# Block-diagonal products of later groups in three one-pass parts, and another way to turn float64 weights into fp32

## The chip, the cores and the metric

The kernel runs on one core of one Trainium2 chip. The metric is the device time of one execution in microseconds (us). The core's engines are PE (matmuls; PEld is its loading of weights), DVE, ACT, POOL (GpSimd) and SP, which here issues the DMAs.

## The reference, cut to what matters

A linear attention block feeds an MLP.

```
kv  = einsum('bhsd,bhse->bhde', k, v)          # (8, 8, 576, 64) inputs
out = einsum('bhsd,bhde->bhse', q, kv)
x   = out / sqrt(mean(out*out, -1) + 1e-6) * g_norm     # -> (4608, 512)
h   = x @ w_in                                  # w_in (512, 2048), float64
g   = h * erf(softplus(h))
y   = g @ w_out                                 # w_out (2048, 512), float64
```

The two weights arrive as float64, two 32-bit words per number. The result is fp32.

## The kernel before, in words

**Groups.** The tokens are handled in nine groups. Groups T = 0 to 7 are the first 512 tokens of each of the eight sequences; the 64 tokens left over from each sequence together make the ninth, T = 8 (`T == B`). The constant FIRST is 2. Heads go in pairs p = 0 to 3: two heads of 64 fill the 128 partitions.

**Attention of one pair** (`attention(T, p)`, L266 and on) is a list of pieces. `products` multiplies k and v into kv_ps (L294), copies the two 64x64 blocks into the block-diagonal matrix bd_kv (L309) and transposes q with PE into qt_ps (L316), which ACT copies to qT in SBUF (L317). `apply` multiplies bd_kv with the tail of q (L321) and with qT (L322, se_ps, an fp32 product), and ACT squares the result (L325). `halve` cuts the square in two fp32r parts (L335, L336). `mean` sums over the heads' rows with PE (L343, L344) and makes the inverse root on ACT by Ln, Exp and Square (L355 to L357); a table load stands ahead of it and one behind it (L103, L106). `norm` makes x with three operations of DVE (L363, L366, L375), the last of which reads se_ps. `split` cuts x into three fp32r forms (L402 on ACT, L405 and L408 on DVE).

**The MLP in three one-pass products.** fp32r products run in one pass. A number is cut into a high and a low part, and a third form holds both with the low part scaled by SHIFT = 4096. `product` (L459) multiplies high by high and low by low into the bank n_ps, and both by both into m_ps; the sum is (SHIFT − 1) n_ps + m_ps, made by one scaled copy from n_ps and one addition of m_ps (L834 on ACT and L442 on DVE for h; L773 or L437 on DVE, and L442, for the result e). `upper`, `lower`, `upper_w` and `lower_w` make these forms; the weights' forms are made once, written to DRAM and read again for each group.

**Stages.** To 29 us: attention of group 0 and the first loads. To about 180 us: group 0's MLP with plain fp32 weights (hidden product L689, result product L517, column n of the 16 hidden columns at a time), while the weights are converted. To about 285 us: group 1, during which the forms of the weights are written out. From there on blocks of 24.9 us: block m = 4T + b takes four hidden columns of group T (the products of `hidden`), then the four result products of the block before it (`result`). The attention of pair b of group T + 1 is threaded in by hand: its pieces are called at the `places` 0 (ahead of the first hidden product), 1 to 4 (behind each of them) and 5 to 8 (behind each result product). Within a block the gates (L873) and the cutting of g (L402, L405, L408 on g_forms) also have fixed places. The program's order is each engine's order: nothing is moved by a scheduler.

**The conversion of the weights** goes in 18 pieces: the first four columns of w_in singly (512 words per partition), the rest of w_in and all of w_out in twos (1024). `load_w` brings a piece to w_raw. `w_split` (L209 to L217) lets ACT scale the upper word, read as fp32, by 2^-112 into w_e (L215), and the lower word by 2^-29 into the integer w_m (L216). `w_join` (L219 to L237) lets DVE shift w_e left by three (L225), put the sign in (L228) and add w_e and w_m as integers (L237); this last is an integer addition that appears in the profile as a custom operation. The pieces of the conversion are called by `weights()` ahead of the column that needs them.

Of the kernel before, what the change touches and what calls it, by code (L numbers as in the profile page):

```python
# [39 lines left out]
FP32 = mybir.dt.float32  # L40
FP32R = mybir.dt.float32r
# [19 lines left out]
def kernel(  # L61
# [110 lines left out]
    for i in range(2):  # L172
        nc.vector.memset(mean_f[i * D : i * D + D, i * D : i * D + D], 1.0 / D)
    nc.vector.tensor_copy(out=mean_w, in_=mean_f)
    eps_col = const.tile([P, 1], FP32, name="eps_col")
    nc.vector.memset(eps_col, EPS)
    bd_kv = const.tile([P, 2, P], FP32, name="bd_kv")
# [19 lines left out]
                in_=moe_w_out.rearrange("(t p) f -> p t f", p=P)[:, f : f + k, :],  # L197
            )

    def words(which, f):  # L200

        raw = w_raw[which, f]
        hi, lo = (
            raw.bitcast(kind).rearrange("p (n two) -> p n two", two=2)[:, :, half]
            for kind, half in ((FP32, 1), (U32, 0))
        )
        return hi, lo, raw.rearrange("p (n two) -> p n two", two=2)[:, :, 1]

    def w_split(which, f, k):  # L209


        hi, lo, _ = words(which, f)
        e = early.tile([P, G * k], I32, name="w_e", tag="w_e", bufs=2)
        m = early.tile([P, G * k], I32, name="w_m", tag="w_m", bufs=2)
        nc.scalar.activation(e.bitcast(FP32), hi, AF.Copy, scale=2.0**-112)  # L215
        nc.scalar.activation(m, lo, AF.Copy, scale=2.0**-29)  # L216
        w_cv[which, f] = e, m  # L217

    def w_join(which, f, k):  # L219


        hi = words(which, f)[2]
        e, m = w_cv.pop((which, f))
        w_raw.pop((which, f))
        nc.vector.tensor_scalar(  # L225
            out=e, in0=e, scalar1=3, scalar2=None, op0=ALU.logical_shift_left
        )
        nc.vector.scalar_tensor_tensor(  # L228
            out=e, in0=hi, scalar=-(1 << 31), in1=e, op0=ALU.bitwise_and, op1=ALU.bitwise_or
        )  # L230
        if which == "in":
            out_ = w_in_sb[:, :, f * P : (f + k) * P]
            e, m = (t.rearrange("p (c f) -> p c f", c=KC) for t in (e, m))
        else:
            out_ = w_out_sb[:, f : f + k, :]
            e, m = (t.rearrange("p (c f) -> p c f", c=k) for t in (e, m))
        nc.vector.tensor_tensor(out=out_.bitcast(I32), in0=e, in1=m, op=ALU.add)  # L237


    w_order = sorted(  # L240
# [25 lines left out]
    def attention(T, p, pools=None):  # L266

        st = {}

        halves = FIRST <= T < B  # L270
        bd = bd_kv[:, (T * NP + p) % 2, :]

        q_tail, o_tail = slice(P, 2 * P), slice(2 * P, 2 * P + R)
# [11 lines left out]
        def products():  # L285

            kv_ps = st["kv"] = bank("kv_ps")
            ks, vs, qs = (x.pop((T, p)) for x in (k_sb, v_sb, q_sb))
            C = chunks(T)
            for c in range(C):  # L290
                rows = slice(0, S // C + (c < S % C))
                for i in range(2):
                    s = slice(i * D, i * D + D)
                    nc.tensor.matmul(  # L294
                        kv_ps[s, s],
                        lhsT=ks[rows, i, c],
                        rhs=vs[rows, i, c],
                        start=(c == 0),
                        stop=(c == C - 1),
                    )  # L300
            if p % 2 == 0:
                nc.tensor.transpose(kv_ps[:, q_tail], q_last[:, p // 2], ident)
            if p == NP - 2:
                for i in range(NP):
                    load_last(T + 1, i)
            st["qT"] = square_tile("qT")
            for i in range(2):
                s = slice(i * D, i * D + D)
                nc.vector.tensor_copy(out=bd[s, s], in_=kv_ps[s, s])  # L309
            if p % 2 == 0:  # L310
                tails[T] = attp.tile([P, P], FP32, name="qT_last", tag="t")
                nc.vector.tensor_copy(out=tails[T], in_=kv_ps[:, q_tail])
            st["tail"] = tails[T][:, p % 2 * R : p % 2 * R + R]
            qt_ps = bank("qt_ps")
            for j in range(J):
                nc.tensor.transpose(qt_ps[:, j * P : j * P + P], qs[:, j], ident)  # L316
            nc.scalar.copy(st["qT"], qt_ps)  # L317

        def apply():
            qT, o_ps, kv_ps = st["qT"], bank("se_ps"), st.pop("kv")  # L320
            nc.tensor.matmul(kv_ps[:, o_tail], lhsT=bd, rhs=st.pop("tail"), start=True, stop=True)  # L321
            nc.tensor.matmul(o_ps, lhsT=bd, rhs=qT, start=True, stop=True)  # L322
            nc.vector.tensor_copy(out=x_last[:, p, T * R : T * R + R], in_=kv_ps[:, o_tail])
            st["o"] = o_ps
            nc.scalar.activation(qT, o_ps, AF.Square)  # L325
# [12 lines left out]
        def mean(table=True):  # L338
            ms = st["ms"] = bank("ms_ps")
            if halves:  # L340


                nc.tensor.matmul(ms, lhsT=mean_w, rhs=st.pop("hi"), start=True, stop=False)  # L343
                nc.tensor.matmul(ms, lhsT=mean_w, rhs=st.pop("lo"), start=False, stop=True)  # L344
                u = square_tile("u")
            else:
                u = st.pop("qT")
                nc.tensor.matmul(ms, lhsT=mean_w.bitcast(FP32), rhs=u, start=True, stop=True)  # L348
            if T > 0:
                r = attp.tile([P, G], FP32, name="rms_r", tag="rms_r")  # L350
                exp_ln_table()
            else:
                r = gate.tile([P, G], FP32, name="rms_r", tag="s")
            st["u"], st["r"] = u, r
            nc.scalar.activation(r, ms, AF.Ln, bias=eps_col)  # L355
            nc.scalar.activation(r, r, AF.Exp, scale=-0.5)
            nc.scalar.activation(u, r, AF.Square)  # L357
            if table and (T > 0 or p == NP - 1):
                softplus_table()

        def norm():
            ms, u, r = (st.pop(name) for name in ("ms", "u", "r"))
            nc.vector.scalar_tensor_tensor(  # L363
                out=u, in0=ms, scalar=EPS, in1=u, op0=ALU.add, op1=ALU.mult
            )
            nc.vector.scalar_tensor_tensor(  # L366
                out=u, in0=u, scalar=3.0, in1=r, op0=ALU.subtract, op1=ALU.mult
            )
            if T < FIRST:
                if T not in xT:  # L370
                    xT[T] = wide.tile([P, KC, G], FP32, name="xT", tag="ab"[T])
                x = xT[T][:, p, :]
            else:
                x = st["x"] = x_new.tile([P, G], FP32, name="x", tag="x")
            nc.vector.scalar_tensor_tensor(  # L375
                out=x,
                in0=st.pop("o"),
                scalar=gm_col,
                in1=u,
                op0=ALU.mult,  # L380
                op1=ALU.mult,
            )
# [9 lines left out]
            return products, apply, halve, mean, norm  # L392
        if T == B:
            return lambda: None, square, lambda: None, mean, norm, split

        pieces = ((products,), (apply,), (halve, loads)) if halves else ((products, loads), (apply,), ())
        return (*(partial(chain, *group) for group in pieces), mean, norm, split)
# [45 lines left out]

    banks = [(ps_h, "h"), (ps_h, "h")] + [(ps_o, f"o{i}") for i in range(4)]

    def product(weights, moving, turns=True):


        n_ps, m_ps = (
            pool.tile([P, G], FP32, name=name, tag=tag)  # L450
            for name, (pool, tag) in zip(("n_ps", "m_ps"), banks[:2])
        )
        if turns:
            banks.extend(banks[:2])
            del banks[:2]
        for ps, forms in ((n_ps, (0, 1)), (m_ps, (2,))):
            for k in range(4):
                for form in forms:
                    nc.tensor.matmul(  # L459
                        ps,  # L460
                        lhsT=weights(form, k),
                        rhs=moving(form, k),
                        start=(form == forms[0] and k == 0),
                        stop=(form == forms[-1] and k == 3),
                    )
        return n_ps, m_ps
# [276 lines left out]

    low_room.close()
    room.close()
    ctx.enter_context(tc.tile_pool(name="shift", bufs=1, side="right")).tile([P, 504], FP32, name="shift")
    late_r = ctx.enter_context(tc.tile_pool(name="late_r", bufs=1, side="right"))
    gate_r = ctx.enter_context(tc.tile_pool(name="gate_r", bufs=1, side="right"))
    w_out_p = ctx.enter_context(tc.tile_pool(name="w_out_p", bufs=7, side="right"))
# [13 lines left out]
    def result(T, b, j, g, w):  # L763
# [5 lines left out]
        if b == 0:  # L769
            if j == 0:  # L770
                all_e = wide.tile([P, J, DM], FP32, name="e", tag="a")
                es.update((i, all_e[:, i]) for i in range(J))
            nc.vector.tensor_scalar(  # L773
                out=es[j], in0=ps[0], scalar1=SHIFT - 1.0, scalar2=None, op0=ALU.mult
            )
        else:
            add_scaled(es[j], ps[0], SHIFT - 1.0)
        add(es[j], ps[1])
# [5 lines left out]
    for m in range(first_batch, batches + 1):  # L784
# [21 lines left out]
                todo[5] = partial(chain, todo[5], softplus_table)  # L806
        elif b == NB - 1:
            places = (0, 2, 3, 5, 6, 7)

        def pieces(place):  # L810
            while todo and places[-len(todo)] <= place:
# [101 lines left out]
```

## Time and profile before

| | |
|---|---|
| median of 16 runs | 981.81 us (980.03 to 984.15) |
| the profiled execution | 981.4 us |
| its span | 979.6 us, 11746 instructions |
| granted PE clock, mean | 0.985 |
| PE busy | 942.1 us, 96% |
| DVE busy | 716.5 us, 73% |
| ACT busy | 617.5 us, 63% |
| DMA | 259.78 MB, mean 265 GB/s |

Times in the profile count from the start of the span. A line of groups names the line of the code, the engine, the operation, output and inputs with partitions by elements; then the number of instructions, their busy time and the mean of one; then the idle time of the engine just before them and what ended it. In a list of windows a stretch is followed by busy time and number of instructions of PE, PEld, DVE, ACT and POOL, and then by the granted PE clock, the DMA engines' share and GB/s. PEclk in the slices is the granted clock in tenths of full speed. A line of waits reads: engine and line, what it waited for, us in total, how often, the longest.

An fp32 128x512 matmul appears as two instructions, and four of them take 3.43 us on the chain; eight one-pass products of fp32r take 1.83 us. Granted clock and PE's waits differ between the early stage and the rest.

### The profile page before, as it was taken

To read this page: it belongs to the slowest core of one execution; us is meant where nothing else is said; L and a number is where in the kernel's file an instruction comes from. 1 tells how busy PE (TensorE), PEld (TensorE's weight loads), DVE (VectorE), ACT (ScalarE), POOL (GpSimd) and SP (SyncE) were. 2 spreads that over 40 slices of the span, in tenths; PEclk is the share of its full clock that TensorE was granted. 3 is DMA by queue.
4 is the path that set the end of the run, shared out by engine and by line. 5 is a ranking of instruction groups with operands and counts; after the bars stand their busy time and mean duration, and the time that the engine had idled before them with its cause. 6 is when DMAs were issued, how large, how long until landed. Compare 5 with 4: busy or idle time off the path is not lost.

```text
span 979.6 us, 11746 instructions
## 1 busy us (share of the span) xinstructions
PE 942.1 (96%) x4272; PEld 687.6 (70%) x4272; DVE 716.5 (73%) x1019; ACT 617.5 (63%) x825; POOL 2.4 (0%) x10
## 2 busy tenths in 40 slices
PE   5578999999999999999999999999999999999997
PEld 4234444566667888887888788777888878888886
DVE  2543654888767888777788787777888877787667
ACT  3665877677666666666666666666666666665551
POOL 0000000000000000000000000000000000000000
PEclk9878999999999999999999999999999999999999
DMA  9754540589979999898988888888888669778871
GB/s 239 238 153 119 169 122 13 208 307 344 327 248 354 311 301 307 282 318 282 300 299 292 292 304 306 290 279 299 288 313 354 257 244 343 266 281 301 335 274 46
DMA packets 111842, 259.78 MB, mean 265 GB/s; under 512 B 43864, under 2 KB 69544, under 8 KB 111784
## 3 DMA queue, kind: packets, MB, share of 16 engines
q1 hardware_dynamic: 110152, 256.73, 76.2%
q10 hardware_dynamic: 1568, 2.29, 0.9%
q8 instruction: 34, 0.56, 0.2%
q14 instruction: 24, 0.20, 0.1%
q0 software_dynamic: 64, 0.00, 0.0%
HBM read 224.40 MB, written 34.60 MB: 264 GB/s over the span
## 4 chain that ended last, share of the span: by engine, by line
PE 86%; DVE 6%; ACT 4%; DMA 2%; issue 1%; SPq 0%; DVEq 0%; ACTq 0%
PE n_ps L459 43%; PE m_ps L459 21%; PE o_ps L517 7%; PE h_ps L689 6%; PE se_ps L322 3%; PE kv_ps L294 2%; PE qt_ps L316 1%; DMA q_last<-in_q_dram 1%; DVE w_e L228 1%; DMA w_in<-w_new 1%; PE ms_ps L348 1%; DMA q_sb<-in_q_dram 1%; DVE w_in_sb L237 1%; ACT w_e L215 1%; DVE h L873 1%
## 5 line engine op out<-in xcount | busy, mean ns | idle before, releaser
L459 PE MATMUL n_ps<-x_forms,w_in_parts 128*128 128x512 f32 x896 | 234.6, 403 | 0.2
L459 PE MATMUL n_ps<-w_out_parts,g_forms 128*128 128x512 f32 x928 | 232.6, 392 | 0.0
L459 PEld LDWEIGHTS n_ps<-w_out_parts,g_forms 128*128 128x128 f32 x928 | 174.2, 188 | 39.7 <-issue 1.7
L459 PEld LDWEIGHTS n_ps<-x_forms,w_in_parts 128*128 128x128 f32 x896 | 166.6, 188 | 45.5 <-issue 10.2
L849 ACT ACTIVATE s<-h 128x512 f32<-128x512 f32 x112 | 71.1, 634 | 177.4 <-DVE h L442 177.4
L459 PE MATMUL m_ps<-w_out_parts,g_forms 128*128 128x512 f32 x464 | 124.4, 390 | 0.0
L442 DVE TENSOR_TENSOR h<-m_ps,h 128x512 f32<-128x512 f32 x116 | 79.7, 687 | 60.7 <-ACT h L834 42.6
L459 PE MATMUL m_ps<-x_forms,w_in_parts 128*128 128x512 f32 x448 | 121.2, 392 | 0.0
L517 PE MATMUL o_ps<-w_out_sb,h_sb 128*128 128x512 f32 x224 | 100.9, 593 | 0.3 <-DVE h_sb L639 0.3
L459 PEld LDWEIGHTS m_ps<-w_out_parts,g_forms 128*128 128x128 f32 x464 | 87.1, 188 | 18.5
L459 PEld LDWEIGHTS m_ps<-x_forms,w_in_parts 128*128 128x128 f32 x448 | 84.1, 188 | 18.9
L689 PE MATMUL h_ps<-xT,w_in_sb 128*128 128x512 f32 x144 | 75.9, 674 | 19.8 <-DVE w_in_sb L237 19.8
L442 DVE TENSOR_TENSOR e<-m_ps,e 128x512 f32<-128x512 f32 x116 | 80.2, 692 | 19.1 <-PE m_ps L459 11.9
L437 DVE SCALAR_TENSOR_TENSOR e<-n_ps,e 128x512 f32<-128x512 f32 x88 | 60.3, 685 | 43.9 <-PE n_ps L459 43.9
L517 PEld LDWEIGHTS o_ps<-w_out_sb,h_sb 128*128 128x128 f32 x224 | 42.5, 191 | 49.4 <-issue 47.0
L408 DVE SCALAR_TENSOR_TENSOR g_forms<-g_forms 128x1024 fp32r<-128x1024 f32 x58 | 71.1, 1225 | 2.0
L689 PEld LDWEIGHTS h_ps<-xT,w_in_sb 128*128 128x128 f32 x144 | 30.1, 215 | 59.7 <-issue 35.3
L405 DVE TENSOR_TENSOR g_forms<-h,g_forms 128x1024 fp32r<-128x1024 f32 x58 | 70.6, 1217 | 1.7 <-ACT g_forms L402 1.4
L834 ACT ACTIVATE h<-n_ps 128x512 f32<-128x512 f32 x112 | 65.5, 585 | 5.3 <-PE n_ps L459 5.3
L873 DVE TENSOR_TENSOR h<-h,s 128x1024 f32<-128x1024 f32 x58 | 68.3, 1218 | 0.6 <-ACT s L853 0.6
L402 ACT ACTIVATE g_forms<-h 128x1024 fp32r<-128x1024 f32 x58 | 58.9, 1060 | 12.7 <-PE m_ps L459 10.0
L106 ACT ACT_TABLE_LOAD x44 | 56.5, 1283 | 0.7
(95 smaller groups left out, 1014.7 us busy)
## 6 DMA issues: line engine op xcount, KB each, us to landing
w_out_parts<-w_out SPq DMA_DIRECT2D x116, 768.0 KB
w_in_parts<-w_in SPq DMA_DIRECT2D x112, 768.0 KB
w_in<-w_new SPq DMA_DIRECT2D x16, 768.0 KB
q_sb<-in_q_dram SPq DMA_DIRECT2D x32, 256.0 KB
w_raw<-in_moe_w_out_dram SPq DMA_DIRECT2D x8, 1024.0 KB
out_dram<-e SPq DMA_DIRECT2D x32, 256.0 KB
k_sb<-in_k_dram SPq DMA_DIRECT2D x28, 287.5 KB
v_sb<-in_v_dram SPq DMA_DIRECT2D x28, 287.5 KB
```

The source lines that it names most:

```text
L106: nc.scalar.preload_act_table_set("softplus")
L402: nc.scalar.activation(high, x, AF.Copy, scale=1.0 + 2.0**-13)
L405: nc.vector.tensor_tensor(out=low, in0=x, in1=high.bitcast(FP32), op=ALU.subtract)
L408: nc.vector.scalar_tensor_tensor(out=both, in0=low.bitcast(FP32), scalar=SHIFT, in1=high.bitcast(FP32), op0=ALU.mult, op1=ALU.add,)
L437: nc.vector.scalar_tensor_tensor(out=out_, in0=ps, scalar=scale, in1=out_, op0=ALU.mult, op1=ALU.add)
L442: nc.vector.tensor_tensor(out=out_, in0=ps, in1=out_, op=ALU.add)
L459: nc.tensor.matmul(ps, lhsT=weights(form, k), rhs=moving(form, k), start=(form == forms[0] and k == 0), stop=(form == forms[-1] and k == 3),)
L517: nc.tensor.matmul(o_ps[j], lhsT=g[:, j * P : j * P + P], rhs=w_out_sb[:, f, :], start=(f == 0), stop=last,)
L689: nc.tensor.matmul(plain[i], lhsT=w_in_sb[:, c, i % FC * P : i % FC * P + P], rhs=xT[T][:, c, :], start=(c == 0), stop=(c == KC - 1),)
L834: nc.scalar.activation(h[:, i], n_ps, AF.Copy, scale=SHIFT - 1.0)
L849: nc.scalar.activation(s[:, i], h[:, i], AF.Softplus)
L873: nc.vector.tensor_tensor(out=part(h, half), in0=part(h, half), in1=part(s, half), op=ALU.mult)
```

## The change

It has four parts. In groups 3 to 7 (the fourth to eighth; `parts`) the product of bd_kv and qT is done like the MLP's, in three one-pass products of cut parts, in two of the banks that the MLP's products turn through. The forms of bd_kv are made by DVE (three operations) in `products`; the copy of qT becomes ACT's `upper`; a new piece `cut` at place 1 lets DVE make the low and the both form; `apply_parts` multiplies, ACT copies (SHIFT − 1) n_ps to a tile o in SBUF, DVE adds m_ps, ACT squares o. `norm` then reads o. In the conversion DVE takes exponent and mantissa out of the upper word, ACT turns them into two floats (Relu with a bias, and Identity), and DVE puts the sign to the exponent's float, adds the lower word scaled by 2^-52 to the mantissa's, and multiplies. In `result` the scaled copy to e in the first block of a group (b == 0) goes from DVE to ACT. The pool `shift` is replaced by the pool of the forms of bd_kv.

```diff
@@ w_split
+        hi = w_raw[which, f].rearrange("p (n two) -> p n two", two=2)[:, :, 1]
-        nc.scalar.activation(e.bitcast(FP32), hi, AF.Copy, scale=2.0**-112)
-        nc.scalar.activation(m, lo, AF.Copy, scale=2.0**-29)
+        nc.vector.tensor_scalar(
+            out=e, in0=hi, scalar1=20, scalar2=0x7FF,
+            op0=ALU.logical_shift_right, op1=ALU.bitwise_and,
+        )
+        nc.scalar.activation(e, e, AF.Relu, scale=float(1 << 23), bias=exp_col)
+        nc.vector.tensor_scalar(
+            out=m, in0=hi, scalar1=0xFFFFF, scalar2=None, op0=ALU.bitwise_and
+        )
+        nc.scalar.activation(m.bitcast(FP32), m, AF.Identity, scale=2.0**-20, bias=1.0)
@@ w_join
-        nc.vector.tensor_scalar(
-            out=e, in0=e, scalar1=3, scalar2=None, op0=ALU.logical_shift_left
-        )
         nc.vector.scalar_tensor_tensor(
             out=e, in0=hi, scalar=-(1 << 31), in1=e, op0=ALU.bitwise_and, op1=ALU.bitwise_or
         )
+        nc.vector.scalar_tensor_tensor(
+            out=m, in0=lo, scalar=2.0**-52, in1=m, op0=ALU.mult, op1=ALU.add
+        )
-        nc.vector.tensor_tensor(out=out_.bitcast(I32), in0=e, in1=m, op=ALU.add)
+        nc.vector.tensor_tensor(out=out_, in0=e, in1=m, op=ALU.mult)
@@ products
+            if parts:
+                kv = st["kv3"] = parts_p.tile([P, 3, P], FP32R, name="kv_forms", tag="kv3")
+                nc.vector.tensor_scalar(
+                    out=kv[:, 0], in0=bd, scalar1=(1.0 + 2.0**-13) / SHIFT, scalar2=None, op0=ALU.mult,
+                )
+                lower_w(bd, *(kv[:, i] for i in range(3)))
...
-            nc.scalar.copy(st["qT"], qt_ps)
+            if parts:
+                x = st["q3"] = [
+                    pool.tile([P, G], FP32R, name=f"q_{name}", tag=tag)
+                    for name, pool, tag in (
+                        ("high", attp, "rms_r"),
+                        ("low", attp, "sq_lo"),
+                        ("both", x_new, "x"),
+                    )
+                ]
+                upper(qt_ps, x[0])
+                st["qt"] = qt_ps
+            else:
+                nc.scalar.copy(st["qT"], qt_ps)
+
+        def cut():
+            lower(st.pop("qt"), *st["q3"])
+
+        def apply_parts():
+            x, w, kv_ps = st.pop("q3"), st.pop("kv3"), st.pop("kv")
+            nc.tensor.matmul(kv_ps[:, o_tail], lhsT=bd, rhs=st.pop("tail"), start=True, stop=True)
+            n_ps, m_ps = two_banks()
+            for i, ps in enumerate((n_ps, n_ps, m_ps)):
+                nc.tensor.matmul(ps, lhsT=w[:, i], rhs=x[i], start=(i != 1), stop=(i != 0))
+            nc.vector.tensor_copy(out=x_last[:, p, T * R : T * R + R], in_=kv_ps[:, o_tail])
+            o = st["o"] = attp.tile([P, G], FP32, name="o", tag="qT")
+            nc.scalar.activation(o, n_ps, AF.Copy, scale=SHIFT - 1.0)
+            add(o, m_ps)
+            st["qT"] = x_new.tile([P, G], FP32, name="sq", tag="x")
+            nc.scalar.activation(st["qT"], o, AF.Square)
@@ attention's list of pieces
+        if parts:
+            return products, cut, apply, partial(chain, halve, loads), mean, norm, split
@@ result
-            nc.vector.tensor_scalar(
-                out=es[j], in0=ps[0], scalar1=SHIFT - 1.0, scalar2=None, op0=ALU.mult
-            )
+            nc.scalar.activation(es[j], ps[0], AF.Copy, scale=SHIFT - 1.0)
@@ the blocks' places
+        if len(todo) > len(places):
+            places = (places[0], 1, *places[1:])
```

The tiles u and x of these groups move to the pool x_new. `two_banks` is the part of `product` that takes two banks, made a function of its own.

More of the change, by code (lines that the diff above doesn't have):

```diff
@@ L174 @@
     nc.vector.tensor_copy(out=mean_w, in_=mean_f)
+    exp_col = const.tile([P, 1], FP32, name="exp_col")
+    nc.vector.memset(exp_col, -896.0 * (1 << 23))
     eps_col = const.tile([P, 1], FP32, name="eps_col")
@@ L198, in load_w @@
             )
[L200 to L205, printed above, removed]
-        )
-        return hi, lo, raw.rearrange("p (n two) -> p n two", two=2)[:, :, 1]
     def w_split(which, f, k):
-        hi, lo, _ = words(which, f)
+        hi = w_raw[which, f].rearrange("p (n two) -> p n two", two=2)[:, :, 1]
         e = early.tile([P, G * k], I32, name="w_e", tag="w_e", bufs=2)
         m = early.tile([P, G * k], I32, name="w_m", tag="w_m", bufs=2)
-        nc.scalar.activation(e.bitcast(FP32), hi, AF.Copy, scale=2.0**-112)
-        nc.scalar.activation(m, lo, AF.Copy, scale=2.0**-29)
+        nc.vector.tensor_scalar(
+            out=e,
+            in0=hi,
+            scalar1=20,
+            scalar2=0x7FF,
+            op0=ALU.logical_shift_right,
+            op1=ALU.bitwise_and,
+        )
[4 more added lines that the diff above has]
+        nc.scalar.activation(m.bitcast(FP32), m, AF.Identity, scale=2.0**-20, bias=1.0)
         w_cv[which, f] = e, m
     def w_join(which, f, k):
[L222 to L225, printed above, removed]
-            out=e, in0=e, scalar1=3, scalar2=None, op0=ALU.logical_shift_left
-        )
+        raw, (e, m) = w_raw.pop((which, f)), w_cv.pop((which, f))
+        hi = raw.rearrange("p (n two) -> p n two", two=2)[:, :, 1]
+        lo = raw.bitcast(U32).rearrange("p (n two) -> p n two", two=2)[:, :, 0]
         nc.vector.scalar_tensor_tensor(
@@ L230, in w_join @@
         )
+        m = m.bitcast(FP32)
+        nc.vector.scalar_tensor_tensor(
+            out=m, in0=lo, scalar=2.0**-52, in1=m, op0=ALU.mult, op1=ALU.add
+        )
+        e = e.bitcast(FP32)
         if which == "in":
@@ L270, in attention @@
         halves = FIRST <= T < B
+        parts = FIRST < T < B
         bd = bd_kv[:, (T * NP + p) % 2, :]
@@ L305, in products @@
                     load_last(T + 1, i)
-            st["qT"] = square_tile("qT")
+            if not parts:
+                st["qT"] = square_tile("qT")
             for i in range(2):
@@ L309, in products @@
                 nc.vector.tensor_copy(out=bd[s, s], in_=kv_ps[s, s])
+            if parts:
+                kv = st["kv3"] = parts_p.tile([P, 3, P], FP32R, name="kv_forms", tag="kv3")
+                nc.vector.tensor_scalar(
+                    out=kv[:, 0],
+                    in0=bd,
+                    scalar1=(1.0 + 2.0**-13) / SHIFT,
+                    scalar2=None,
+                    op0=ALU.mult,
+                )
+                lower_w(bd, *(kv[:, i] for i in range(3)))
             if p % 2 == 0:
@@ L316, in products @@
                 nc.tensor.transpose(qt_ps[:, j * P : j * P + P], qs[:, j], ident)
-            nc.scalar.copy(st["qT"], qt_ps)
+            if parts:
[25 more added lines that the diff above has]
+            nc.scalar.activation(st["qT"], o, AF.Square)
         def apply():
+            if parts:
+                return apply_parts()
             qT, o_ps, kv_ps = st["qT"], bank("se_ps"), st.pop("kv")
@@ L344, in mean @@
                 nc.tensor.matmul(ms, lhsT=mean_w, rhs=st.pop("lo"), start=False, stop=True)
-                u = square_tile("u")
+                u = (
+                    x_new.tile([P, G], FP32, name="u", tag="x")
+                    if parts
+                    else square_tile("u")
+                )
             else:
@@ L372, in norm @@
                 x = xT[T][:, p, :]
+            elif parts:
+                x = st["x"] = u
             else:
@@ L394, in attention @@
             return lambda: None, square, lambda: None, mean, norm, split
+        if parts:
+            return products, cut, apply, partial(chain, halve, loads), mean, norm, split
         pieces = ((products,), (apply,), (halve, loads)) if halves else ((products, loads), (apply,), ())
@@ L444, with two_banks @@
     banks = [(ps_h, "h"), (ps_h, "h")] + [(ps_o, f"o{i}") for i in range(4)]
-    def product(weights, moving, turns=True):
-        n_ps, m_ps = (
+    def two_banks(turns=True):
+        ps = [
             pool.tile([P, G], FP32, name=name, tag=tag)
             for name, (pool, tag) in zip(("n_ps", "m_ps"), banks[:2])
-        )
+        ]
         if turns:
@@ L455, in product @@
             del banks[:2]
+        return ps
+    def product(weights, moving, turns=True):
+        n_ps, m_ps = two_banks(turns)
         for ps, forms in ((n_ps, (0, 1)), (m_ps, (2,))):
@@ L745 @@
     room.close()
-    ctx.enter_context(tc.tile_pool(name="shift", bufs=1, side="right")).tile([P, 504], FP32, name="shift")
+    parts_p = ctx.enter_context(tc.tile_pool(name="parts_p", bufs=1, side="right"))
     late_r = ctx.enter_context(tc.tile_pool(name="late_r", bufs=1, side="right"))
@@ L772, in result @@
                 es.update((i, all_e[:, i]) for i in range(J))
-            nc.vector.tensor_scalar(
-                out=es[j], in0=ps[0], scalar1=SHIFT - 1.0, scalar2=None, op0=ALU.mult
-            )
+            nc.scalar.activation(es[j], ps[0], AF.Copy, scale=SHIFT - 1.0)
         else:
```

## The prediction

> **What bounds the kernel now.** I read the engine shares and the slices first, then the windows by stage, then PE's and DVE's waits, last the order of one block. The page:
>
> ```profile
> PE 942.1 (96%) x4272; PEld 687.6 (70%) x4272; DVE 716.5 (73%) x1019; ACT 617.5 (63%) x825; POOL 2.4 (0%) x10
> ...
> PEclk9878999999999999999999999999999999999999
> ...
> PE 86%; DVE 6%; ACT 4%; DMA 2%; issue 1%; SPq 0%; DVEq 0%; ACTq 0%
> ```
>
> PE is busy 96% of the span and makes 86% of the chain that ends last. That is a mean over two different stages, as the windows show (columns: stretch, then busy time of PE, PEld, DVE, ACT):
>
> ```profile
> 29.00:180.00 151.00, 131.21 (x393) 59.22 (x392) 77.75 (x105) 99.97 (x130) 0.00 (x0) 0.91 0.42 132
> ...
> 300.50:500.00 199.50, 199.50 (x1014) 160.26 (x1013) 159.91 (x228) 126.65 (x168) 0.00 (x0) 1.00 0.90 301
> ```
>
> From 300.5 us on, PE never idles: 8 blocks in 199.5 us, 24.94 us a block, with 20.0 of DVE and 15.8 of ACT in each. In the early stage (group 0's MLP while the weights are converted) PE is busy 131 of 151 us, and what it lacks has one name:
>
> ```profile
> PE h_ps L689 <- DVE w_in_sb L237: 19.8, 5, 6.6
> ```
>
> So the change meets two stages with different limits: the conversion is awaited by PE, the block-diagonal product is in a stage where PE is full. The question there is how much room DVE and ACT have, and a busy share of 80% does not answer it. Their order within a block does:
>
> ```profile
> 358.41 0.68 DVE L437 SCALAR_TENSOR_TENSOR e<-n_ps,e 128x512 f32<-128x512 f32 x1
> ...
> 362.52 0.45 DVE L309 COPY bd_kv<-kv_ps 64x64 f32<-64x64 f32 x2
> 363.00 1.23 DVE L405 TENSOR_TENSOR g_forms<-h,g_forms 128x1024 fp32r<-128x1024 f32 x1
> ...
> 368.52 0.68 DVE L442 TENSOR_TENSOR h<-m_ps,h 128x512 f32<-128x512 f32 x1
> ...
> 370.87 0.69 DVE L442 TENSOR_TENSOR h<-m_ps,h 128x512 f32<-128x512 f32 x1 [1.54 <-ACT h L834]
> ...
> 372.75 0.69 DVE L442 TENSOR_TENSOR h<-m_ps,h 128x512 f32<-128x512 f32 x1
> ```
>
> ```profile
> 369.24 0.63 ACT L849 ACTIVATE s<-h 128x512 f32<-128x512 f32 x1 [1.87 <-DVE h L442]
> ...
> 373.47 0.63 ACT L849 ACTIVATE s<-h 128x512 f32<-128x512 f32 x1 [0.76 <-DVE h L442]
> 374.12 1.28 ACT L853 ACT_TABLE_LOAD   x1
> 375.42 2.01 ACT L853 ACTIVATE s<-s 128x1024 f32<-128x1024 f32 x2
> ```
>
> Follow the round from one x (L375, ends 358.50) to the next. DVE runs without a gap from 358.41 to 369.2; ACT's softplus at 369.24, its square (369.78) and its copy of h (370.25) then hold DVE's next add to 370.87; DVE goes on to 373.44; ACT then runs softplus, table load, two erfs, table load (377.44 + 1.30), logarithm 0.72, exponential 0.66, square 0.65 and releases u at 380.77; the norm's three operations (0.72, 0.73, 0.75) end x at 382.97. That **round is 24.5 us and does not go through PE; PE's period is 24.94.** DVE does wait for PE (below), but while ACT walks from softplus to u, where the wait costs nothing:
>
> ```profile
> DVE e L437 <- PE n_ps L459: 14.2, 12, 1.6
> DVE h L442 <- ACT h L834: 12.3, 8, 1.5
> ```
>
> So 0.4 us of a block is all the room there is for work put into this round.
>
> **The parts product (20 pairs).** On PE it removes the fp32 128x512 product (two instructions, 0.91 us on the chain, from 1.83 for two pairs) and adds three one-pass ones (0.229 each, 0.69; eight take 1.83): 0.22 us less. The wait of PE's kv matmul for x (L375; 6.7 us in 19 times, it shares the bank of se_ps) goes as well, 0.35 a block. On DVE and ACT, all in the round:
> - kv_forms, three 128x128 operations behind the bd copies. Rows: 64x64 copies 0.22, 128x128 copy from PSUM 0.29. I take 0.28, +0.85; bounds 0.66 to 0.87.
> - The cut at place 1: q_low (as L405 128x512, pitch 0.61) and q_both (as L408, 0.72) stand between the first add of h and the second cut of g: +1.33. `upper` replaces the copy of qT, same engine and shape: 0.
> - o leaves PSUM by an ACT copy (0.59, as L834) and a DVE add (0.69, as L442) before the square can start. Softplus, copy, add, square, copy of h, add of h are one chain: +1.35 with the handoffs. Behind the waiting add stand the third add of h and the sq_hi cast; the softplus waits for those. The loads keep their place behind the halves: SP's order of issues is the same before and after.
>
> Sum +3.53: **the round becomes 28.0 us**, bound by DVE and ACT; PE idles about 3 us a block at the three one-pass products, which wait for q_both. The opposite bound is nothing, if all of it fell into DVE's waits; but DVE shows no gap between 358.41 and 369.2, which excludes that for the first two.
>
> **The e copies on ACT (one block in four, b = 1).** Before, DVE scales the four e (L773, 0.69). After, ACT's order is: second erf, e0, table load, logarithm, exponential, u, softplus table load, e1, e2, e3. The add of e1 stands ahead of the gates (2 x 1.17) and the norm on DVE. So x waits for u, then table 1.30, e1 0.59, add 0.69, gates 2.35, then the norm; with e0 0.59 ahead of u that is about +5.4: **33.4 us**. The next round lacks two DVE operations (the scalings of e2 and e3, pitch 0.79 each): 26.5. Other end: 0, if the gates were already through; the order of the instructions excludes it, so I put it below as a rival.
>
> Per group: 28.05 + 33.4 + 26.5 + 28.05, and 0.24 twice for the copy of the q tails (even pairs) = 116.5, against 4 x 24.94 = 99.75: +16.8, times 5 groups = **+84**. Group 8's blocks keep their attention but have the e copies: about +3. The ninth group's blocks have no attention: 0.
>
> **The clock.** In the early stage the granted clock was 0.50 in 50–54 and 70–76 us, after idles of 6.6 and 4.6 us, and there 6 instructions took 5.49 us instead of 2.57; even after 2.1 us idle 6 took 4.54. New idles of 3 us per block may bring the same: +1.7 to 2.9 us of slower matmuls, but beside a round that has some 3 us of slack on PE; between 0 and +0.6 a block, up to +13; I take 0. The Trainium skill ("TensorE: Matmul & The Clock Gate", section "HAM oscillation — how this bites in real kernels") warns of idle gaps above about 3.4 us; by it the new idles of about 3 us would cost nothing, while this trace shows half clock after idles of 2.1 and 2.5 us.
>
> **The conversion.** PE loses 19.8 us waiting, and about 11.7 more to the slow clock behind these idles (8.91 and 8.17 us for 14 instructions of 0.43; 5.49, 4.31 and 4.54 for 6): 31 in all. The five waits are for the join of a *later* piece than the one that is multiplied: the custom join writes w_in_sb as one range over all c, so column n waits for joins whose range only spans it. The ordinary multiply of the new join frees PE from that. Against it, DVE's part of a piece grows. Its rows:
>
> ```profile
> L228 DVE SCALAR_TENSOR_TENSOR w_e<-w_raw,w_e 128x1024 int32<-128x1024 int32 x14 | 17.1, 1225 | 0.5
> L237 DVE CUSTOM_DVE_ANT_0 w_out_sb<-w_e,w_m 128x2048 uint16<-128x2048 uint16 x8 | 9.8, 1226 | 1.1
> L225 DVE TENSOR_SCALAR w_e<-w_e 128x1024 int32<-128x1024 int32 x14 | 9.6, 689 | 18.5 <-ACT w_e L215 18.4
> ```
>
> Before: 0.69 + 1.23 + 1.23 = 3.14 us per large piece. After: two tensor_scalars that read every second word, two scalar_tensor_tensors and a multiply, 3 x 1.23 = 3.68, plus 2 x 0.69 (nearest row L225, same kind and type, but not strided) = 5.05, or 2 x 1.22 if striding costs what L228's strided read shows = 6.1. Over 14 large and 4 small pieces: +31 to +48 us of DVE work, in a stage where DVE has 73 us idle (151 − 77.75). ACT's two operations per piece stay at two; the first now waits for DVE. Walked in order, the last matmul of column 16 falls at about 155 us at 1.22 and 142 to 147 at 0.69, where now it ends at 170.85: gain 12 to 16, or 24 to 29. I take **−20**; bounds −4 (DVE the bound in the stage) and −29 (nearly all of the 31).
>
> The Trainium skill ("VectorE: DVE Perf Modes", section "What auto-detection actually checks") lets a single-source operation with source and destination in SBUF run twice as fast, with no demand on the inner step for 32-bit types; by it the price would be 0.69. No row of this trace has the strided form.
>
> **Sum.** −20 + 84 + 3 = +67 on the profiled execution's 981.4 us (span 979.6 and 1.8 around it): 1048. The median of the runs is 981.8, so the forecast is **1048 us**, slower by 6.8%.
>
> **Rivals.**
> - *PE stays the bound, faster.* If the added operations fit beside PE, each of the 20 blocks shortens by 0.22 + 0.35 = 0.57, −11, and the early stage gives −20: **950** (939 to 967). It decides at the round from x to x: below 24.4 us it wins. For it: DVE is busy only 80%, ACT 63%. Against it: the idle of both is waiting for each other.
> - *The e copies cost nothing.* Then b = 1 is an ordinary block, 4 x (28.05 − 24.94) + 0.48 = 12.9 a group, +65 − 20: **1026**.
> - *The early stage gains nothing*, because DVE's 48 us more become its bound: 84 + 3 − 4 = **1065**.
> - *The clock follows every new idle:* +13: **1061**.
> - *The waits do not go*, because the new join is still tracked over the whole range: then as the third, up to 1078 with DVE's work late.
>
> **Numbers.** Forecast (1039 to 1056 by the two walks of the conversion) 0.5; e copies free 0.12; no early gain 0.14; clock 0.12; PE stays the bound, or the round has enough unseen slack to come out below 980, 0.10; in between (the round half hidden) 0.02. The range is 1004 to 1078: low takes −29, the e copies free (+65) and half of o's detour hidden (20 x 0.67 = −13), so 981.4 + 23; high takes −4 + 84 + 3 + 13, so 981.4 + 96. It leaves out the PE rival. A difference of 0.2% (2 us) is what can be told from no change. Faster 0.09, same 0.02, slower 0.89.
>
> **What would show it.** Block time about 28 us from 285 to 785 us and 33 for b = 1, instead of 24.9; PE waiting some 3 us a block for q_low and q_both ahead of the new product; DVE waiting for the copies of e (about 4 us, five times) and for o; PE's wait for w_in_sb gone or below 8 us, and the first fp32r product of group 1 (now at 183.7 us) some 20 us earlier. I am wrong if PE stays 100% busy past 300 us, if PE's slices keep DVE's additions out of the round, or if group 1 starts no earlier.

## The result, and the profile after

The changed kernel takes **1037.04 us** (median of 8 runs, 1035.98 to 1038.00) against 981.48 us of the kernel before in the same comparison: ratio 1.0566, 95% interval 1.0554 to 1.0579. Its profiled execution has a span of 1035.1 us, 55.5 us more than before.

The page of the changed kernel, the lines that answer to those of before:

```profile
PE 961.4 (93%) x4292; PEld 703.6 (68%) x4292; DVE 778.0 (75%) x1148; ACT 642.2 (62%) x873; POOL 2.4 (0%) x10
...
PEclk9999999999989999999998999999999999999999
...
PE 58%; DVE 25%; ACT 9%; issue 5%; DMA 2%; SPq 1%; DVEq 0%; ACTq 0%
```

The 8, 7, 8 of the granted clock near the start are gone, and two slices further on have an 8. The busy shares moved by 3 points at most, but PE's share of the chain that ends last fell from 86% to 58%, and DVE's and ACT's together rose from 10% to 34%: another loop sets the pace.

The windows of the changed kernel, the early stage and the 20 blocks that carry the pairs of groups 3 to 7 (the columns are stretch; busy time of PE, PEld, DVE, ACT, POOL; granted clock, DMA share, GB/s):

```profile
29.00:151.00 122.00, 121.30 (x397) 56.09 (x396) 103.56 (x139) 99.00 (x131) 0.00 (x0) 1.00 0.52 168
...
270.90:851.26 580.36, 525.79 (x2518) 417.94 (x2517) 436.40 (x658) 339.26 (x459) 0.00 (x0) 0.96 0.75 255
```

The early stage is now full on PE at a clock of 1.00. The blocks, full on PE before, now leave PE idle for 55 of 580 us. PE's waits in the changed kernel name the places:

```profile
PE n_ps L354 <- DVE q_low L459: 40.3, 19, 2.7
...
PE h_ps L747 <- DVE w_in_sb L240: 0.6, 1, 0.6
```

Marks that both kernels have (the first one-pass product of group 1; the first erf of a block) divide the difference:

| stretch | before, us | after, us | difference | forecast |
|---|---|---|---|---|
| to the first one-pass product of group 1 | 183.1 | 151.3 | −31.8 | −20 |
| from there to the erf of the first block, which carries the first pair | 117.2 | 119.6 | +2.4 | in the next line |
| the next 20 blocks | 498.3 | 580.4 | +82.1 | +84 with the line above |
| four blocks of the eighth group (T = 7; "group 8" in the forecast) | 92.9 | 96.8 | +3.9 | +3 |
| the rest (the ninth group) | 88.1 | 87.1 | −1.1 | 0 |
| span | 979.6 | 1035.1 | +55.5 | +67 |

The blocks' own period, from erf to erf, goes 28.0, 31.9, 28.4, 28.2 us through a typical group, where it was 24.8 to 25.1 in most (up to 25.5).

### The profile page after: what moved, and what is told of

Same layout as the page of the kernel before. It is cut to its first block, busy times and chain, and to the rows that moved or that the text cites. A ratio compares the mean times of both kernels' runs of the same rounds, so it can differ in the third digit from the quotient of the medians.

```text
span 1035.1 us, 12031 instructions
## 1 busy us (share of the span) xinstructions
PE 961.4 (93%) x4292; PEld 703.6 (68%) x4292; DVE 778.0 (75%) x1148; ACT 642.2 (62%) x873; POOL 2.4 (0%) x10
## 4 chain that ended last, share of the span: by engine, by line
PE 58%; DVE 25%; ACT 9%; issue 5%; DMA 2%; SPq 1%; DVEq 0%; ACTq 0%
PE n_ps L517 26%; PE m_ps L517 12%; PE o_ps L575 9%; PE h_ps L747 5%; DVE e L496 3%; DVE g_forms L459 3%; DVE h L931 3%; DVE h L496 3%; ACT s L911 2%; DVE e L491 2%; PE kv_ps L298 1%; ACT s L907 1%; DVE x_forms L459 1%; DVE q_both L462 1%; DVE q_low L459 1%
## 5 line engine op out<-in xcount | busy, mean ns | idle before, releaser
L517 PE MATMUL n_ps<-x_forms,w_in_parts 128*128 128x512 f32 x896 | 242.8, 416 | 1.9 <-DVE x_forms L459 0.8
L517 PEld LDWEIGHTS n_ps<-x_forms,w_in_parts 128*128 128x128 f32 x896 | 178.7, 201 | 43.3 <-DVE x_forms L459 1.6
L517 PE MATMUL m_ps<-x_forms,w_in_parts 128*128 128x512 f32 x448 | 125.2, 402 | 0.8 <-DVE e L496 0.8
L496 DVE TENSOR_TENSOR h<-m_ps,h 128x512 f32<-128x512 f32 x116 | 79.7, 687 | 54.1 <-ACT h L892 34.3
L517 PEld LDWEIGHTS m_ps<-x_forms,w_in_parts 128*128 128x128 f32 x448 | 87.4, 195 | 21.2 <-DVE e L496 1.2
L517 PEld LDWEIGHTS m_ps<-w_out_parts,g_forms 128*128 128x128 f32 x464 | 87.1, 188 | 18.3
L747 PE MATMUL h_ps<-xT,w_in_sb 128*128 128x512 f32 x144 | 64.8, 594 | 0.7 <-DVE w_in_sb L240 0.6
L911 ACT ACTIVATE s<-s 128x1024 f32<-128x1024 f32 x56 | 56.2, 1052 | 0.3
```

The costliest lines, as they stand in the source:

```text
L496: nc.vector.tensor_tensor(out=out_, in0=ps, in1=out_, op=ALU.add)
L517: nc.tensor.matmul(ps, lhsT=weights(form, k), rhs=moving(form, k), start=(form == forms[0] and k == 0), stop=(form == forms[-1] and k == 3),)
L747: nc.tensor.matmul(plain[i], lhsT=w_in_sb[:, c, i % FC * P : i % FC * P + P], rhs=xT[T][:, c, :], start=(c == 0), stop=(c == KC - 1),)
L911: nc.scalar.activation(part(s, i), part(s, i), AF.Erf)
```

## The experiments

The theory: there are two effects that add. The early stage gains because the matmuls no longer wait for the joins of later pieces; the blocks lose because the round from x to x through DVE and ACT, 24.5 us before, became 28 and longer in every fourth block. The rivals: PE's new wait for q_low is itself the loss; DVE is simply too full; the conversion gains by its new operations.

### The conversion alone, and its last operation

Three kernels take the conversion apart. The first is the kernel before with the new `w_split` and `w_join` alone.

> Only the new conversion is put into the kernel before; products of the attention and the copies of e stay. Main theory: the conversion's gain stands in the early stage alone and shifts all that follows rigidly, 183.1 to 151.3 us at the first one-pass product of group 1, so 981.5 - 32 = 949 to 951 us; blocks stay at 24.9 us. Rival: part of the 32 us is used up again by later stages that now start on other terms (transfers of the weights' forms): 960 or more.

Measured: 944.68 us (944.16 to 945.32), ratio 0.962 (0.960 to 0.964). The first one-pass product of group 1 falls at 151.13 us, as in the changed kernel. The gain is 37 us, 5 more than forecast; the last experiment below shows where these come from. **This kernel beats both others, by 3.8% and by 8.9%.**

The second has the same five operations of DVE and two of ACT per piece, and only makes the last one the integer addition again:

```diff
-        nc.scalar.activation(m.bitcast(FP32), m, AF.Identity, scale=2.0**-20, bias=1.0)
+        nc.scalar.activation(m, m, AF.Copy, scale=8.0)
...
-            out=m, in0=lo, scalar=2.0**-52, in1=m, op0=ALU.mult, op1=ALU.add
+            out=m, in0=lo, scalar=2.0**-29, in1=m, op0=ALU.mult, op1=ALU.add
...
-        nc.vector.tensor_tensor(out=out_, in0=e, in1=m, op=ALU.mult)
+        nc.vector.tensor_tensor(out=out_.bitcast(I32), in0=e, in1=m, op=ALU.add)
```

> As the conversion alone, with the same number of operations of DVE and ACT per piece, but the last operation is again the integer addition that the profile shows as a custom operation (ACT scales the mantissa by 8, DVE adds the lower word by 2^-29, and e and m are added as integers). Theory of the tracked range: matmuls wait again for the join of a later piece, the idles of PE and the half clock behind them return, and since DVE has five operations per piece instead of three they are no shorter: 981 us or more, up to 1000. Rival (the gain comes from what ACT and DVE do per piece): 950 us like the conversion alone.

Measured: 982.9 us (ratio 1.0005, 0.9994 to 1.0016), 38 us more than with the multiplication; the first one-pass product falls at 188.9 us. PE's waits in it:

```profile
PE h_ps L690 <- DVE w_in_sb L238: 26.5, 5, 8.0
```

Five waits, as before the change, and a little longer, as DVE does more per piece.

The third goes the other way: the kernel before, with one word changed.

```diff
-        nc.vector.tensor_tensor(out=out_.bitcast(I32), in0=e, in1=m, op=ALU.add)
+        nc.vector.tensor_tensor(out=out_.bitcast(I32), in0=e, in1=m, op=ALU.bitwise_or)
```

> The kernel before with one word changed: the join's integer addition becomes a bitwise or, an ordinary operation (this alters the mantissas of weights whose rounding carries, so the output is only near the reference's). Three operations of DVE per piece. Theory of the tracked range: the waits for later joins go, 949 to 953 us. Rival: the pace of ACT and DVE per piece sets the waits, then nothing changes: 981 us.

Measured: 953.82 us (952.73 to 954.91), ratio 0.971; the first one-pass product at 153.3 us, and no wait of PE for w_in_sb among its waits. So the kind of the last operation decides the early stage in both directions, and the work of DVE and ACT per piece does not. That the custom operation's write is taken for one unbroken range is read from the program's waits (each of the five matmuls waits for a piece that it doesn't use) and stays an inference; the runs show that the wait hangs on this operation.

### The two stages add

The changed kernel with the conversion of before:

> The changed kernel with the conversion of before. Main theory: the two stages add, 1037 + 32 = 1067 to 1070 us, with blocks of 28.0 to 28.8 us as in the changed kernel. Rival (they interact): 1050 or less.

Measured: 1067.86 us (1066.27 to 1069.05). Blocks are 28.0 to 28.7 us with 31.9 to 32.8 in every fourth, as in the changed kernel. The old conversion costs 30.8 us here, where the early stage alone differed by 31.8: within about 1 us the two parts add.

### What sets the blocks

First, is it PE's wait for q_low? The piece `cut` goes ahead of the first cut of g:

```diff
-            places = (places[0], 1, *places[1:])
+            places = (places[0], 0, *places[1:])
```

> The changed kernel with the cut of q moved from place 1 to place 0, ahead of the first cut of g. Theory of the round through DVE and ACT: DVE has the same operations in the round, so the time stays within 3 us of 1037, though PE's wait for q_low (40.3 us) shrinks to below 10; PE then waits elsewhere. Rival (PE's wait for q_low is what the blocks lose): about 995 to 1005 us.

Measured: 1033.64 us (1031.72 to 1034.29). PE's waits in this kernel:

```profile
PE qt_ps L331 <- DVE u L412: 22.2, 5, 4.5
PE m_ps L517 <- DVE h L496: 9.1, 14, 0.7
...
PE n_ps L354 <- DVE q_low L459: 5.0, 10, 0.6
```

The wait of 40.3 us shrank to 5.0 and the time by 3.4 only, just beyond the 3 that were allowed: PE waits elsewhere for the same round. The ordinary blocks now repeat to 0.01 us, at 28.01 (28.19 or 28.20 where the q tails are copied). **The round, not the wait that shows in it, is the bound.**

Second, does PE's work still count? The three matmuls of a pair are issued twice:

```diff
-            for i, ps in enumerate((n_ps, n_ps, m_ps)):
+            for i, ps in 2 * tuple(enumerate((n_ps, n_ps, m_ps))):
```

> The changed kernel with the three one-pass matmuls of each of the 20 pairs issued twice (0.69 us more of PE a block). Theory of the round: PE has about 3 us of slack a block, so 1037 to 1040 us. Rival (PE still bounds): +14, 1051 us.

Measured: 1042.0 us (1040.86 to 1042.91), 5 more, a third of the rival's 14 but 2 above the expected range. Several blocks are unchanged (28.01, 28.20, 31.86), other ordinary ones are up to 29.5, and one long one takes 33.4; so PE's work is mostly, not wholly, covered.

Third, does DVE's work in the round count one for one? The three operations on kv_forms twice:

> The changed kernel with the three DVE operations of kv_forms issued twice in each of the 20 pairs (0.84 us more of DVE a block). Theory of the round: all of it shows, +16 to +18: 1053 to 1055 us. Rival (DVE, busy 75%, has room): 1037 to 1041 us.

Measured: 1061.24 us (1060.71 to 1062.33), +24, more than the theory said. Ordinary blocks go from 28.92, about what was expected, to 30.75. In PE's timeline of this kernel, the block of 30.75:

```profile
383.34 0.79 PE L362 MATMUL n_ps<-q_low,kv_forms 128*128 128x512 f32 x1 [2.46 <-DVE q_low L467]
...
384.65 3.62 PE L525 MATMUL n_ps<-x_forms,w_in_parts 128*128 128x512 f32 x8
388.07 1.91 PE L525 MATMUL m_ps<-x_forms,w_in_parts 128*128 128x512 f32 x4
```

The eight matmuls behind the idle take 3.62 us, where the same eight take 2.03 earlier in the block: the granted clock is 0.50 from 383.0 to 389.8 us, behind 2.46 us of idle, and the hidden product that DVE and ACT need next is late. So with the cut at place 0, where PE's longest wait for q_low is 0.6 us, the same doubling should cost only its own time:

> The changed kernel with kv_forms issued twice and the cut at place 0. Theory (the round costs 0.84 to 0.9 us a block, and the rest of what the doubling cost at place 1 is PE's slow clock behind its wait for q_low): against the 1033.6 us of the cut at place 0, +17 to +18, 1051 to 1052 us, with ordinary blocks of 28.9 us. Rival (the doubled operations cost 1.2 us a block wherever PE waits): 1057 to 1058 us.

Measured: 1050.25 us (1049.79 to 1050.62), 16.6 above the 1033.64 and just under the expected range; ordinary blocks are 28.91 or 28.92, +0.91 each. The other 7.6 us of the 24.2 (6.6 in the profiles of the 20 blocks) go with the slow clock. Set side by side from one x to the next, the kernel with the doubling at place 1 has 11 blocks that are longer than the same ones at place 0, by 0.15 to 1.65 us, 11.4 in sum; each of the 11 holds a stretch of granted clock 0.50, and the blocks without such a stretch agree to 0.03 us. For the changed kernel against the cut at place 0 it is 8 blocks and 4.8 us, in the same way.

Fourth, the detour of o. DVE's addition is taken out:

```diff
-            add(o, m_ps)
```

> The changed kernel without DVE's addition of m_ps to o: the sum of the cross terms is left out of the attention's product, so the output is off. Theory of the round: softplus, copy of o, square, copy of h follow on ACT without a trip to DVE, 0.7 to 0.8 us less in each of 20 blocks: 1021 to 1024 us. Rival (the addition lies beside DVE's waits): 1036 to 1038 us.

Measured: 1023.24 us (1022.11 to 1026.86), −14, in the expected range; ordinary blocks 27.28 to 27.30 where nothing disturbs them, 0.72 less than 28.01.

### The copies of e

The changed kernel with the copies of e back on DVE, and the kernel before with only these copies on ACT:

```diff
-            nc.vector.tensor_scalar(
-                out=es[j], in0=ps[0], scalar1=SHIFT - 1.0, scalar2=None, op0=ALU.mult
-            )
+            nc.scalar.activation(es[j], ps[0], AF.Copy, scale=SHIFT - 1.0)
```

> The changed kernel with the scaled copies of e back on DVE. Theory of the round: the long blocks (31.9 us) become ordinary ones (28.0 to 28.5), -4.2 for each of five groups, -3.9 in group 8's blocks and +1.1 in the ninth's: 1010 to 1015 us. Rival: DVE is the scarce engine and each of the 28 operations put back costs its 0.69 us: 1037 to 1056 us.

Measured: 1017.81 us (1017.53 to 1018.48), −19. DVE got 28 operations back and the kernel became faster, so DVE is not simply too full. The long blocks became ordinary ones, but the ordinary ones still scatter from 28.0 to 28.9, which is 3 us more than the expectation allowed.

> The kernel before with only the scaled copies of e moved from DVE to ACT. Theory of the round: a b = 1 block takes 24.5 + 5.4 = 29.9 us and the next 24.5 - 1.6 = 22.9 at DVE, PE's period makes that 24.9 in part, so +3 to +5 for each of six groups: 998 to 1010 us, with DVE waiting about 5 us for ACT e in each. Rival: DVE is relieved by 0.69 us four times and nothing is lost, 977 to 982 us.

Measured: 1012.67 us (1011.7 to 1013.7), ratio 1.031 (1.029 to 1.033): +31, at the upper end and a little over. The b = 1 blocks took 29.9 to 30.8 us and the next 25.2. Moving four short copies per group off the busier engine costs 3% by itself, on a kernel that is otherwise unchanged.

### One constant more

The conversion alone had blocks of 24.78 us and gained 5 us there, though nothing in its blocks was changed; so had the version with the integer addition, and not the one with the bitwise or. What the first two have and the third lacks is exp_col:

```diff
+    exp_col = const.tile([P, 1], FP32, name="exp_col")
+    nc.vector.memset(exp_col, -896.0 * (1 << 23))
```

> The kernel before with nothing but the extra constant column exp_col (one float per partition and its memset at the start), which moves the tiles that are allocated behind it by a few bytes. The kernels that have it beside the old products show steady blocks of 24.78 us instead of 24.8 to 25.1. Theory of the layout: the addresses do it, so 976 to 977.5 us, with the early stage as before. Rival (the new operations of the conversion do it): 981 to 982 us.

Measured: 975.73 us (973.77 to 976.50), ratio 0.9942 (0.9924 to 0.9960). Early stage as before (first one-pass product at 183.5 us), blocks of 24.8. That is just under the expected range, and the 5.6 us cover the 5 that were left open above.

## Why the prediction was right, point by point

The measured 1037.04 us lie 11 below the 1048 that were forecast, inside the range, and 2 below the 1039 to 1056 that held half of the chances. Nearly all of the distance is the early stage's.

**The round: right.** The 24.5 us of before end at 382.97, a sum; in the trace this x (L375, 382.51 + 0.75) ends at 383.26, 24.76 after the one before it, because the gates, behind additions that wait for PE, run to about 381.1, past the end of u. So 24.5 is the round without PE, as was meant, and the sentence that these waits cost nothing is off by 0.3 there. The walk said 28.05 us. With the slow clock out of the way the blocks take 28.01 (28.19 or 28.20 with the tails). A full group was put at 116.5 us; that kernel's groups take 28.01 + 31.86 + 28.01 + 28.19 = 116.1. DVE in an ordinary block of the changed kernel:

```profile
460.55 0.23 DVE L317 TENSOR_SCALAR kv_forms<-bd_kv 128x128 fp32r<-128x128 f32 x1
...
464.47 0.68 DVE L459 TENSOR_TENSOR q_low<-qt_ps,q_high 128x512 fp32r<-128x512 f32 x1
465.18 0.69 DVE L462 SCALAR_TENSOR_TENSOR q_both<-q_low,q_high 128x512 fp32r<-128x512 f32 x1
465.79 1.22 DVE L459 TENSOR_TENSOR g_forms<-h,g_forms 128x1024 fp32r<-128x1024 f32 x1
...
468.79 0.21 DVE L355 COPY x_last<-kv_ps 128x64 f32<-128x64 f32 x1
470.05 0.69 DVE L496 TENSOR_TENSOR o<-m_ps,o 128x512 f32<-128x512 f32 x1 [1.05 <-ACT o L357]
471.93 0.69 DVE L496 TENSOR_TENSOR h<-m_ps,h 128x512 f32<-128x512 f32 x1 [1.19 <-ACT h L892]
```

From 460.55 the kv_forms take 0.80 until g is cut at 461.35 (0.85 was said). The cut of q goes from 464.47 to 465.79, 1.32 (1.33). From the copy of x_last to the next addition of h it was 1.75 us before (369.12 to 370.87) and is 3.14 now (468.79 to 471.93): 1.39 (1.35). The copy in the kernel before:

```profile
369.12 0.21 DVE L323 COPY x_last<-kv_ps 128x64 f32<-128x64 f32 x1
```

In sum 3.51 us were added, and 3.53 were said.

**The copies of e: right.** 33.4 + 26.5 = 59.9 was said for the long block and the next, from x to x. From erf to erf they take 31.86 + 28.01 = 59.9, since the mark erf comes ahead of the copies and the mark x behind them. From x to x, in the kernel with the cut at place 0, they take 33.27 and 26.60:

```profile
395.20 0.75 DVE L426 SCALAR_TENSOR_TENSOR u<-o,gm_col,u 128x512 f32<-128x512 f32 x1
...
428.47 0.75 DVE L426 SCALAR_TENSOR_TENSOR u<-o,gm_col,u 128x512 f32<-128x512 f32 x1
...
455.07 0.75 DVE L426 SCALAR_TENSOR_TENSOR u<-o,gm_col,u 128x512 f32<-128x512 f32 x1
```

DVE's additions in the changed kernel, and ACT's side of it:

```profile
418.73 0.69 DVE L496 TENSOR_TENSOR e<-m_ps,e 128x512 f32<-128x512 f32 x1 [4.50 <-ACT e L831]
423.97 0.69 DVE L496 TENSOR_TENSOR e<-m_ps,e 128x512 f32<-128x512 f32 x1 [4.55 <-PE m_ps L517]
```

```profile
418.13 0.58 ACT L831 ACTIVATE e<-n_ps 128x512 f32<-128x512 f32 x1
418.72 1.28 ACT L103 ACT_TABLE_LOAD   x1
...
422.05 1.28 ACT L106 ACT_TABLE_LOAD   x1
423.34 1.58 ACT L831 ACTIVATE e<-n_ps 128x512 f32<-128x512 f32 x3
```

The second wait is put down to PE, whose m_ps for that product was done by 419.2; the copy that starts at 423.34 behind the table load and ends at about 423.9 is what the addition at 423.97 waited for. The name in brackets is a guess by order of time; the other engine's rows settle it.

**The early stage: right in mechanism, too small.** The term that was sized too small is "I take −20; bounds −4 and −29": measured −31.8, all of what PE had lost there (19.8 of waits and about 11.7 of slow clock), and past the bound. The last matmul of column 16 ends at 139.0 us, where the walk gave 142 to 147 at the faster rate. The doubt was whether DVE's 31 to 48 us more would become the bound and at what rate the strided reads run. They run at the contiguous rate:

```profile
L207 DVE TENSOR_SCALAR w_e<-w_raw 128x1024 int32<-128x1024 int32 x14 | 9.6, 687 | 0.1
L216 DVE TENSOR_SCALAR w_m<-w_raw 128x1024 int32<-128x1024 int32 x14 | 9.6, 687 | 0.0
```

0.687 us against 0.689 of L225, and not the 1.22 that the operations with two sources take. This agrees with what the Trainium skill states ("VectorE: DVE Perf Modes", section "What auto-detection actually checks"). DVE had 103.6 us to do in 122, so it kept ahead of PE. Those 11.8 us are the distance between the +67 of the sum and the +55.5 of the spans; what is off elsewhere nearly cancels.

**The clock: between the ends.** 0 was taken, up to +13 allowed. The slow clock cost 4.8 us in the 20 blocks (580.4 against 575.6 us with the cut at place 0; 3.4 in the medians), since PE's slack mostly covers it; with less slack (kv_forms twice) it cost 11.4 (604.2 against 592.8; 11.0 in the medians). That the blocks came to +84.5, where +84 was said, is therefore partly luck: with the cut at place 0 the same stretch is only 79.7 longer than before, so the round was priced about 4 too high and the clock about 5 too low. Of the 4, 2 are the group's 116.1 for 116.5; where the others lie was not followed. The prediction puts the half clock at 50 to 54 us behind the idle of 6.6 us; that idle ends at 38.03, and the one just ahead of 50 to 54 is of 4.0. The rule of the Trainium skill that was weighed ("TensorE: Matmul & The Clock Gate", section "HAM oscillation — how this bites in real kernels", idle gaps above about 3.4 us) does not hold as a lower limit here: with kv_forms twice, idles of 2.46 us (shown above) and of 1.87 us (another block, ending at 446.68) were followed by eight matmuls in 3.62 and 3.48 us instead of 2.03.

**The eighth group and the rest:** +3 was said for the copies of e in the eighth group, +3.9 measured; the ninth group, put at 0, became 1.1 shorter; its blocks carry no attention, so no norm stands behind the copies.

**The rivals.** "PE stays the bound" fell: 20 blocks are 82 us longer, and PE's work doubled at the product costs a third of what it would. (The 0.35 us a block in that rival's sum is no wait of PE: the 6.7 us belong to PEld, and PE's own list before has no wait for x.) "The e copies cost nothing" fell by 19 and 31 us in two kernels. "No early gain" and "the waits do not go" fell with the first wait list above.

## What to carry to other kernels

Before putting work on an engine that is "75% busy", follow the round that its instructions make with the other engines, from one result to the same one a period later: if that is within 2% of the period (24.5 of 24.94 here), every operation added inside it lengthens the period by its own time, and what PE saves comes to nothing. Moving an operation to the idler engine is no relief when a table load or a waiting instruction stands ahead of it in that engine's order. And where a matmul waits for a writer of data that it does not read, look at the kind of operation that writes: changing one operation gave 28 to 38 us.

## What the runs showed of the hardware beyond that

One float per partition more among the constants made the whole kernel 0.6% faster. A hidden product in the kernel before, and then in the kernel that has only this constant more (PE's timelines):

```profile
437.73 2.03 PE L459 MATMUL n_ps<-x_forms,w_in_parts 128*128 128x512 f32 x8
439.59 1.09 PE L459 MATMUL m_ps<-x_forms,w_in_parts 128*128 128x512 f32 x4
440.52 0.33 PE L321 MATMUL kv_ps<-qT_last,bd_kv 128*128 128x64 f32 x2
```

```profile
436.98 1.98 PE L461 MATMUL n_ps<-x_forms,w_in_parts 128*128 128x512 f32 x8
438.79 1.08 PE L461 MATMUL m_ps<-x_forms,w_in_parts 128*128 128x512 f32 x4
439.71 0.33 PE L323 MATMUL kv_ps<-qT_last,bd_kv 128*128 128x64 f32 x2
```

From the start of the product to the next matmul it is 2.79 us in the first and 2.73 in the second, for the same twelve instructions. The constant moves the tiles allocated behind it; that their addresses are the reason is inferred from this, and which tile it is was not tried. In the changed kernel a difference of this size does not show, as PE has slack in its blocks: they take 580.4 us with the constant and 579.2 in the kernel with the conversion of before, which lacks it.
